# A routed mixture of experts whose block loop is reordered in three places: the planner's frames, the code's arms, and two small blocks' transposes

## The chip, the cores and the metric

The kernel runs on one core of a Trainium2 chip. The metric is device time of the whole program in microseconds (us). PE is the matmul engine, PEld its weight loads, DVE the vector engine, ACT the scalar engine, POOL GpSimd, SP the engine that issues most DMAs.

## What is computed

```python
# attention: b=8 batches, 12 heads, 448 rows, 64 columns
scores = scale * np.matmul(q, k.transpose(0, 1, 3, 2)) - np.log(S)
attn = 1.0 / (1.0 + np.exp(-scores))
x = rows_of(np.matmul(attn, v))          # 3584 x 768
# experts: 8 of them, 768 -> 1024 -> 768
do_compute = x @ w_skip > 0
xc = x[do_compute]
e_idx = np.argmax(xc @ w_gate, axis=1)   # one expert for each row
gate_w = softmax(xc @ w_gate)[e_idx]
for e in range(E):
    h = np.maximum(xc[e_idx == e] @ w1[e], 0.0)
    y[e_idx == e] = gate_w * (h @ w2[e])
out = x.copy(); out[do_compute] = xc + y
```

With these inputs 1333 rows go to experts, by the reference's own arithmetic 36, 12, 0, 158, 17, 675, 19 and 416 to experts 0 to 7.

## The kernel before

**Stages.** The first 300 us are the attention and the routing, batch by batch; while the last batches run, the weights of the fullest expert (expert 7) are loaded and split. Two blocks of expert 7 run outside a loop, a planner on DVE (L857 to L1031) works out a table of the other blocks meanwhile, and a loop over that table (L1443) runs them one after the other.

**Blocks.** A full block is 128 rows of one expert. Its matmuls take each weight as the sum of two parts: `wh`, a rounded copy that ACT makes (`hi1`, `hi2`), and `wl`, the remainder that DVE and POOL make (`lo1`, `lo2`). Activations are split in the same way (`hh` on ACT L523, `hl` on DVE L524). So a full block has 98 matmuls of one pass. A small block has at most 64 rows and multiplies with the unsplit weights `raw`: `half` (33 to 64 rows) and `few` (up to 32). An expert whose rows fill no full block is called pure, and has one small block and no other. An expert with full blocks is called mixed, and its remainder, if it has one, is a small block as well, ahead of its first full block.

**Two sets of weights.** `raw` holds the next expert, `wh` and `wl` the one whose full blocks run. The last full block of a mixed expert is a splitting block: it multiplies with the old `wh` and `wl`, and as each is read for the last time, it overwrites it with the parts of `raw`. It is of type SPLIT where the next mixed expert has a remainder, which still needs `raw`, and of type LAST where it has none, and then issues the loads of the next `raw` itself. A small block issues the loads of the next `raw` behind its own matmuls (`load_w1` behind the first product, `load_w2` behind the second), from SP. Pure experts are put one to a frame behind the full blocks, so that each finds its `raw` loaded.

**Frames.** The planner gives every full block a number, `slot`. A frame is a slot's remainder block, full block and pure block in this order. `gs` is the slot of a mixed expert's first full block, `prk` a pure expert's place among the pure ones, and `pf` the frame that a pure expert gets.

**Rows ahead.** While a block runs, its rows are in `xc`, those of the next in `xn`, and those of the one behind that are gathered from the output in DRAM to `xg` by POOL (`fetch`). A block ends in `finish` (DVE writes `ys`), `put` (POOL: a tiny `jk` that reads `xg`, and then the scatter of `ys` to the output) and `advance` (DVE copies `xn` to `xc`, `xg` to `xn`, and the records). A gather waits until the scatter ahead of it has landed, `jk` and `advance` wait until the gather has landed. `turn_x` transposes `xn` on PE in two halves of three matmuls, into `pxt[0]` and `pxt[1]`; `ready_x` splits them.

**Arms.** The loop's body reads the block's type on every engine and branches to one of five arms, each with its own code on each engine. With all the steps in the arms written out in order by hand (`manual_schedule`), the order on each engine is that of the code.

**Blocks of this run.** In the trace of before the loop runs: full, SPLIT (both expert 7), half (remainder of 5), full, half (expert 0), full, few (1), full, few (4), full, few (6), SPLIT (all full ones of expert 5), few (remainder of 3), full (3). That is the order that the planner's lines give for the counts above.

Of the kernel before, what the change touches and what calls it, by code (L numbers as in the profile page):

```python
# [15 lines left out]
ALU = mybir.AluOpType  # L16
AX = mybir.AxisListType
# [7 lines left out]
def kernel(  # L25
# [451 lines left out]
    def turn_x(x, h, px):  # L477
        for j in range(3):
            i = 3 * h + j
            nc.tensor.transpose(  # L480
                px[:, j * P : (j + 1) * P], x[:, i * P : (i + 1) * P], ident
            )
# [326 lines left out]
    xn = rows_pool.tile([P, DM], F32, name="xn")  # L809
# [25 lines left out]
    FULL, SPLIT, LAST, FEW, HALF = range(5)  # L835
# [8 lines left out]
    def small(name, w=NE, dt=F32):  # L844
        return area(w, dt)

    def dep(t, e):
        return t.unsqueeze(2).to_broadcast([P, NE, NE]) if e else t.unsqueeze(1).to_broadcast([P, NE, NE])
# [6 lines left out]
    V = nc.vector  # L855
# [28 lines left out]
    mixed = small("mixed")  # L884
# [13 lines left out]
    bef = area(NE * NE).rearrange("p (e f) -> p e f", e=NE)  # L898
# [8 lines left out]
        gemm2(j, hh0, hl0, py)  # L907


    tmp = small("tmp")  # L910
    V.scalar_tensor_tensor(tmp, gs, 3.0, mixed, op0=ALU.is_le, op1=ALU.mult)
    soon = small("soon", 1)
    V.tensor_reduce(soon, tmp, axis=AX.X, op=ALU.add)
    late = small("late")
    V.scalar_tensor_tensor(late, gs, 3.0, mixed, op0=ALU.is_gt, op1=ALU.mult)
    push = small("push")
    V.tensor_tensor(push, gs, mrk, op=ALU.subtract)
    V.tensor_scalar(push, push, soon, -4.0, op0=ALU.add, op1=ALU.add)
    V.tensor_tensor(bef, dep(push, 0), dep(prk, 1), op=ALU.is_le)
    V.tensor_tensor(bef, bef, dep(late, 0), op=ALU.mult)  # L920
    pf = small("pf")
    V.tensor_reduce(pf, bef, axis=AX.X, op=ALU.add)
    V.scalar_tensor_tensor(pf, pf, 3.0, prk, op0=ALU.add, op1=ALU.add)


# [337 lines left out]
    def few(i):  # L1263

        nx = next_expert(ds(i + 2, 1))

        def quarter(dst, g, n, a, w, j, most):
            nc.tensor.matmul(  # L1268
                dst[g * SM : (g + 1) * SM, :n],
                a,  # L1270
                w,
                start=(j == 0),
                stop=(j == most - 1),
                tile_position=(0, g * SM),
            )

        Q1 = FF // 4
        for j in range(NK1):
            for g in range(4):
                s = slice((g % 2) * Q1, (g % 2 + 1) * Q1)  # L1280
                quarter(ph[0], g, Q1, xf[:, j, :SM], raw1[j][g // 2][:, s], j, NK1)
        turned = (pht[0], ph[1])
        parts = [slice(c * P, (c + 1) * P) for c in range(2)]
        for s in parts:
            nc.scalar.activation(hs[:, s], ph[0][:, s], AF.Relu)
        for j in range(NK1):
            for h in range(2):
                load_w1(j, h, nx)
        fetch()
        turn_x(xn, 0, pxt[0])  # L1290
        ht4 = ht[:, : 8 * SM].rearrange("p (c g t) -> p c g t", c=2, g=4)
        for s, p in zip(parts, turned):
            nc.tensor.transpose(p[:, :P], hs[:, s], ident)
        for s, p in zip(parts, turned):
            nc.scalar.activation(ht[:, s], p[:, :P], AF.Copy)
        turn_x(xn, 1, pxt[1])
        shift(pool)
        ready_x()

        for n, j in enumerate((0, 2, 1, 3)):  # L1300
            for g in range(4):
                o, h = g // 2, g % 2
                m = j + h * (NK2 // 2)
                quarter(
                    py[:, 0, :],
                    g,
                    H2,
                    ht4[:, j % 2, 2 * h + j // 2, :],
                    raw2[m][:, o * H2 : (o + 1) * H2],
                    n,  # L1310
                    NK2 // 2,
                )
        for j in range(NK2 // 2):
            for g in range(2):
                load_w2(j + g * (NK2 // 2), nx)
        for g in range(4):
            o, m = divmod(g, 2)
            s = slice(o * H2, (o + 1) * H2)
            nc.vector.scalar_tensor_tensor(
                ys[:SM, s],  # L1320
                py[g * SM : (g + 1) * SM, 0, :H2],
                recs[:SM, 0, 0:1],
                (ys if m else xc)[:SM, s],
                op0=ALU.mult,
                op1=ALU.add,
            )
        put(SM)
        advance()

    def half(i):  # L1330
# [21 lines left out]
            for h in range(2):  # L1352
                load_w1(j, h, nx)
        fetch()
        turn_x(xn, 0, pxt[0])
        for c in range(4):
            nc.tensor.transpose(
                turned[c // 2][:, (c % 2) * P : (c % 2 + 1) * P],
# [2 lines left out]
            )  # L1361
        for s, p in zip(parts, turned):
            nc.scalar.activation(ht[:, s], p[:, : 2 * P], AF.Copy)
        turn_x(xn, 1, pxt[1])
        ready_x()
        shift(dve)

# [38 lines left out]
    def choose(kind, i, todo):  # L1406

        if len(todo) == 1:
            with tc.manual_schedule():
                arms[todo[0]](i)  # L1410
            return
        n = 1 if FULL in todo else (len(todo) + 1) // 2
        with tc.If(kind < todo[n]) as c:
            choose(kind, i, todo[:n])
        with c.Else():
            choose(kind, i, todo[n:])
# [31 lines left out]
```

## Time and profile before

| | |
|---|---|
| median of 3 runs | 582.51 us (580.81 to 585.02) |
| profiled execution | 585.59 us, its span 583.9 us |
| granted clock, mean | 0.979 |
| PE busy | 530.6 us, 91% of the span |
| DMA, mean over the span | 174 GB/s |

The profiled execution is 3.1 us above the median; its span leaves 1.7 us of it out. The loop's first block starts at 346.24 us of the span, its last matmul ends at 569.35 us. Times below are of this one execution.

### The profile page before, as it was taken

The page shows a single profiled execution, that of the slowest core. Times are in us where ns is not written, and L with a number is a line of the kernel's source. Part 1 is how long each engine was busy: PE and PEld are TensorE (multiplying, and loading weights), DVE is VectorE, ACT ScalarE, POOL GpSimd, SP SyncE. Part 2 cuts the span into 40 slices and gives each one's busy share as a digit, 9 for nine tenths or more (in the row PEclk, how much of TensorE's full clock was granted, in tenths as well). Part 3 has the DMA queues.
Part 4 walks back from the last instruction along what each step waited for, and adds up shares of the span by engine and source line. Part 5 has one row for each costly group of instructions (what it writes and reads, how often), then busy time and mean ns, then how long its engine had stood idle before and what let it go on. Part 6 is the DMA issues. An engine that isn't in the chain of part 4 may idle for free.

```text
span 583.9 us, 15458 instructions
## 1 busy us (share of the span) xinstructions
PE 530.6 (91%) x4803; PEld 347.7 (60%) x4804; DVE 322.7 (55%) x716; ACT 273.0 (47%) x473; POOL 263.0 (45%) x377
## 2 busy tenths in 40 slices
PE   7989999999999999888889999799999999997790
PEld 6654544544445454443448898575859686776490
DVE  3555748466485666857948621386341435439732
ACT  4766666766667576664551122182222222257120
POOL 2524543353433536669774222086332334347630
PEclk9999999999999999999999999799999999998896
DMA  8899797687966869999951229119385869593100
GB/s 213 173 250 200 153 191 163 136 159 152 203 147 138 176 139 213 218 216 218 234 113 18 98 63 363 38 59 317 135 294 203 275 217 314 213 331 132 35 14 28
DMA packets 138361, 101.46 MB, mean 174 GB/s; under 512 B 98132, under 2 KB 113764, under 8 KB 138304
## 3 DMA queue, kind: packets, MB, share of 16 engines
q1 hardware_dynamic: 132240, 91.58, 61.4%
q0 software_dynamic: 4032, 8.65, 4.8%
q10 hardware_dynamic: 2032, 0.50, 0.4%
q8 instruction: 32, 0.52, 0.4%
q14 instruction: 25, 0.20, 0.1%
HBM read 92.64 MB, written 17.86 MB: 189 GB/s over the span
## 4 chain that ended last, share of the span: by engine, by line
PE 54%; DMA 15%; issue 10%; DVE 7%; ACT 6%; POOL 3%; SPq 2%; ACTq 0%; DVEq 0%; POOLq 0%
PE s L209 15%; PE pa L237 13%; PE py L531 7%; PE ph L504 6%; DMA out_dram<-ys,rp 5%; ACT at L229 5%; DMA xg<-out_dram,rp 5%; PE b_ph L504 3%; PE b_py L531 3%; DMA out_dram<-y 2%; PE pl L277 1%; SPq L260 1%; PE ph L1268 1%; DMA wr<-in_moe_w_dram 1%; SPq L169 1%
## 5 line engine op out<-in xcount | busy, mean ns | idle before, releaser
L229 ACT ACTIVATE at<-s,bias 128x896 f32<-128x896 f32 x192 | 172.3, 913 | 97.3 <-PE s L209 96.7
L209 PE MATMUL s<-x 64*64 64x448 f32 (+1 forms) x1536 | 166.1, 498 | 14.4 <-ACT at L229 4.7
L237 PE MATMUL pa<-at,v 64*64 64x448 f32 (+1 forms) x1536 | 163.6, 491 | 0.0
L176 POOL COPY kq<-kq 32x896 f32<-32x896 f32 (+1 forms) x96 | 87.8, 914 | 120.3 <-DMA kq<-in_q_dram 80.8
L209 PEld LDWEIGHTS s<-x 64*64 64x64 f32 x1536 | 79.1, 191 | 75.3 <-issue 30.4
L237 PEld LDWEIGHTS pa<-at,v 64*64 64x64 f32 x1536 | 60.7, 133 | 56.0 <-issue 49.8
L194 DVE STREAM_TRANSPOSE x<-kq 128x448 f32<-128x448 f32 x94 | 81.5, 941 | 8.0 <-POOL kq L176 7.2
L247 DVE TENSOR_TENSOR xt<-xt,pa 128x448 f32<-128x448 f32 x48 | 29.7, 618 | 67.6 <-ACT xt L642 62.5
L407 POOL DMA_INDIRECT lst<-rec,idx x32 | 31.4, 982 | 28.0 <-DVE idx L402 14.9
L513 ACT ACTIVATE hs<-ph 128x512 f32<-128x512 f32 x16 | 9.5, 596 | 62.6 <-PE ph L504 61.2
L531 PE MATMUL py<-wh,hl 128*128 128x384 f32 x128 | 33.3, 341 | 4.4 <-DVE hl L524 4.4
L252 DVE STREAM_TRANSPOSE y<-xt 128x448 f32<-128x448 f32 x48 | 31.0, 645 | 10.8 <-DMA out_dram<-y 9.4
L504 PE MATMUL ph<-wh,xh 128*128 128x512 f32 x96 | 29.7, 411 | 6.2 <-issue 5.7
L531 PE MATMUL py<-wh,hh 128*128 128x384 f32 x128 | 34.2, 348 | 0.0
L531 PE MATMUL py<-wl,hh 128*128 128x384 f32 x128 | 32.8, 337 | 0.0
L474 POOL TENSOR_TENSOR wl<-wr,wh 128x384 fp32r<-128x384 f32 (+1 forms) x28 | 31.0, 1133 | 3.0 <-DVE wh L473 1.6
L547 POOL DMA_INDIRECT xg<-out_dram,rp x14 | 14.8, 1056 | 38.8 <-DMA out_dram<-ys,rp 36.8
L504 PE MATMUL ph<-wl,xh 128*128 128x512 f32 x96 | 30.7, 411 | 0.0
L524 DVE TENSOR_TENSOR hl<-pht,hh 128x512 fp32r<-128x512 f32 x16 | 11.1, 691 | 33.1 <-ACT hh L523 28.1
L504 PE MATMUL ph<-wh,xl 128*128 128x512 f32 x96 | 27.9, 399 | 0.0
L1185 POOL TENSOR_TENSOR jk<-ys,xg 128x2 f32<-128x2 f32 (+2 forms) x14 | 4.6, 328 | 51.5 <-DVE ys L542 38.0
L504 PEld LDWEIGHTS ph<-wh,xh 128*128 128x128 f32 x96 | 18.3, 195 | 14.1 <-issue 10.4
(263 smaller groups left out, 734.2 us busy)
## 6 DMA issues: line engine op xcount, KB each, us to landing
raw<-in_moe_w_dram SPq DMA_DIRECT2D x84, 256.0 KB
raw<-in_moe_w_dram SPq DMA_DIRECT2D x56, 384.0 KB
v<-in_v_dram SPq DMA_DIRECT2D x48, 256.0 KB
out_dram<-y SPq DMA_DIRECT2D x192, 56.0 KB
kq<-in_k_dram SPq DMA_DIRECT2D x46, 224.0 KB
kq<-in_q_dram SPq DMA_DIRECT2D x46, 224.0 KB
wr<-in_moe_w_dram SPq DMA_DIRECT2D x12, 256.0 KB
wr<-in_moe_w_dram SPq DMA_DIRECT2D x16, 192.0 KB
```

Of the source, the lines that this page charges most:

```text
L176: nc.gpsimd.tensor_copy(a[BT:, :, :, :BT], a[:BT, :, :, BT:])
L194: nc.vector.transpose(xs[:, n].rearrange("p (r j) -> p j r", j=NJ), t.rearrange("p (j d) -> p j d", d=D)[:, :, :BT],)
L209: nc.tensor.matmul(sc[m * D : (m + 1) * D, j, : qs.stop - qs.start], xs[r, 0, first::NR7], xs[r, 1, qs], start=True, stop=True,)
L229: nc.scalar.activation(at[:, :, :n], sc[:, :, :n], AF.Sigmoid, bias=bias, scale=SCALE)
L237: nc.tensor.matmul(pa[j * D : (j + 1) * D, r, qs], vt[rs, j, r + c if c < 3 else 3 * (1 - r), :], at[rs, j, : qs.stop - qs.start], start=( ...
L247: nc.vector.tensor_tensor(x, x, pa[:, 1, :S], op=ALU.add)
L252: nc.vector.transpose(y, xts[b][:, hp, :])
L407: put = nc.gpsimd.indirect_dma_start(out=lst[:, :], out_offset=bass.IndirectOffsetOnAxis(ap=idx[:, c : c + 1], axis=0), in_=rec[:, c, :], ...
L474: nc.gpsimd.tensor_tensor(lo, r, hi, op=ALU.subtract)
L504: nc.tensor.matmul(ph[h], a[:, j * P : (j + 1) * P], w[j][h], start=(n == 0), stop=(n == len(t) - 1),)
L531: nc.tensor.matmul(py[:, o, :H2], a[h][:, js], w[j][:, o * H2 : (o + 1) * H2], start=(j == 0 and n == 0), stop=(j == NK2 - 1 and n == 2),)
L547: nc.gpsimd.indirect_dma_start(out=dst, out_offset=None, in_=out[0:rows, :], in_offset=bass.IndirectOffsetOnAxis(ap=idx, axis=0), bounds_c ...
```

## The change

**Planner.** Before, a pure expert goes into the frame `3 + prk` plus one for every mixed expert (that starts behind slot 3) whose first slot has been reached by then, so that frames are skipped one at a time: the count `pf` is a sum. After, each such mixed expert pushes pure experts by an amount `away` of its own, which is worked out so that none stands in the frame ahead of a splitting block, and the largest push counts: `pf` is a maximum. With the counts above, experts 0, 1, 4 and 6 stand in frames 4, 5, 6 and 7 before, and in 4, 5, 6 and 9 after. The loop's blocks are then: full, SPLIT, half (5), full, half (0), full, few (1), full, few (4), full, SPLIT, few (3), full (3), few (6). The small block of expert 6 leaves the place ahead of the second splitting block and becomes the last block. The planner has five DVE instructions more.

**Arms.** The type is compared in another order, and the true side is always placed next. The arms stand in each engine's code as FULL, SPLIT, few, half, LAST before, and as SPLIT, FULL, LAST, few, half after; the loop's end stands behind them all.

**Transposes.** In `few` and `half` both halves of `turn_x` stand ahead of the transposes of `hs`, instead of one ahead and one behind.

```diff
+    at4 = small("at4")
+    V.scalar_tensor_tensor(at4, gs, 4.0, mixed, op0=ALU.is_equal, op1=ALU.mult)
+    held = small("held", 1)
+    V.tensor_reduce(held, at4, axis=AX.X, op=ALU.add)
+    V.scalar_tensor_tensor(held, soon, 2.0, held, op0=ALU.mult, op1=ALU.add)
     push = small("push")
-    V.tensor_tensor(push, gs, mrk, op=ALU.subtract)
-    V.tensor_scalar(push, push, soon, -4.0, op0=ALU.add, op1=ALU.add)
+    V.scalar_tensor_tensor(push, mrk, -2.0, gs, op0=ALU.mult, op1=ALU.add)
+    V.tensor_scalar(push, push, held, -5.0, op0=ALU.add, op1=ALU.add)
+    away = small("away")
+    V.scalar_tensor_tensor(away, push, -1.0, gs, op0=ALU.mult, op1=ALU.add)
+    V.scalar_tensor_tensor(away, away, -3.0, late, op0=ALU.add, op1=ALU.mult)
     V.tensor_tensor(bef, dep(push, 0), dep(prk, 1), op=ALU.is_le)
-    V.tensor_tensor(bef, bef, dep(late, 0), op=ALU.mult)
+    V.tensor_tensor(bef, bef, dep(away, 0), op=ALU.mult)
     pf = small("pf")
-    V.tensor_reduce(pf, bef, axis=AX.X, op=ALU.add)
+    V.tensor_reduce(pf, bef, axis=AX.X, op=ALU.max)
     V.scalar_tensor_tensor(pf, pf, 3.0, prk, op0=ALU.add, op1=ALU.add)
...
         fetch()
-        turn_x(xn, 0, pxt[0])
+        for h in range(2):
+            turn_x(xn, h, pxt[h])
...
             nc.scalar.activation(ht[:, s], p[:, :P], AF.Copy)
-        turn_x(xn, 1, pxt[1])
...
-        n = 1 if FULL in todo else (len(todo) + 1) // 2
-        with tc.If(kind < todo[n]) as c:
+        if todo[0] == FULL:
+
+            with tc.If(kind > FULL, preferred_fallthrough_block=True) as c:
+                choose(kind, i, todo[1:])
+            with c.Else():
+                choose(kind, i, todo[:1])
+            return
+        n = (len(todo) + 1) // 2
+        with tc.If(kind < todo[n], preferred_fallthrough_block=True) as c:
             choose(kind, i, todo[:n])
```

On PE, at the end of the first arm in the code and the start of the next (`py` is the second product, `ph` the first; L1413 is the branch). Before, this is FULL and then SPLIT:

```order
L531 MATMUL py<-wh_7_123,hh_4361 128x384 x2
L531 MATMUL py<-wl_7_131,hh_4361 128x384 x2
L531 MATMUL py<-wh_7_123,hl_4363 128x384 x2
L1413 UNCONDITIONAL_BRANCH
L1413 COMPARE_AND_BRANCH x2
L504 MATMUL ph_4372<-wh_0_0_92,xh 128x512
L504 MATMUL ph_4372<-wl_0_0_104,xh 128x512
L504 MATMUL ph_4372<-wh_1_0_94,xh 128x512
```

After, the same place holds SPLIT's end and FULL's start, and SPLIT is what the loop's head runs into without a taken branch:

```order
L531 MATMUL py<-wh_7_123,hh_4366 128x384 x2
L531 MATMUL py<-wl_7_131,hh_4366 128x384 x2
L531 MATMUL py<-wh_7_123,hl_4368 128x384 x2
L1429 UNCONDITIONAL_BRANCH
L504 MATMUL ph_4377<-wh_0_0_92,xh 128x512
L504 MATMUL ph_4377<-wh_1_0_94,xh 128x512
L504 MATMUL ph_4377<-wh_2_0_96,xh 128x512
```

Two arms changed places; a SPLIT multiplies by `wh` and `wl` in turn, a FULL by all `wh` first. The whole code of LAST now stands between FULL and `few`, where SPLIT stood.

On PE in `few`, between its two products (`pxt` are the halves of the next rows, `pht` and `ph_4373` the transposes of `hs`, L1268 the products). Before:

```order
L480 MATMUL pxt_4294<-ident,xn 128x128 x3
L1293 REGISTER_ALU
L1293 MATMUL pht<-ident,hs 128x128
L1293 REGISTER_ALU
L1293 MATMUL ph_4373<-ident,hs 128x128
L480 MATMUL pxt_4295<-ident,xn 128x128 x3
L1268 ISA
L1268 MATMUL py<-raw_0_4352,ht 32x384
```

After:

```order
L480 MATMUL pxt_4299<-ident,xn 128x128 x3
L480 MATMUL pxt_4300<-ident,xn 128x128 x3
L1303 REGISTER_ALU
L1303 MATMUL pht<-ident,hs 128x128
L1303 REGISTER_ALU
L1303 MATMUL ph_4378<-ident,hs 128x128
L1277 ISA
L1277 MATMUL py<-raw_0_4357,ht 32x384
```

The second half's three transposes moved from behind the two of `hs` to ahead of them, in `half` likewise.

## Rows read from the trace of the kernel before

**Rows 1.** The page: busy us, share of the span, instructions.

```profile
PE 530.6 (91%) x4803; PEld 347.7 (60%) x4804; DVE 322.7 (55%) x716; ACT 273.0 (47%) x473; POOL 263.0 (45%) x377
```

**Rows 2.** Windows: stretch, length, busy us (instructions) by engine, PEclk, DMA share, GB/s.

```profile
369.29:390.19 20.90, 20.90 (x99) 18.36 (x99) 11.14 (x16) 13.42 (x26) 8.86 (x11) 0.87 0.09 25
369.29:375.17 5.88, 5.88 (x14) 4.63 (x15) 0.00 (x0) 0.00 (x0) 0.00 (x0) 0.52 0.05 16
480.46:488.44 7.98, 7.00 (x90) 4.15 (x89) 4.01 (x11) 2.69 (x12) 2.20 (x7) 1.00 0.73 225
507.02:515.40 8.38, 7.00 (x89) 4.15 (x89) 4.08 (x12) 2.69 (x12) 2.21 (x7) 1.00 0.64 208
515.40:538.65 23.25, 19.91 (x98) 17.63 (x98) 16.66 (x25) 14.05 (x27) 15.69 (x21) 0.93 0.67 237
538.65:550.93 12.28, 8.07 (x89) 4.10 (x89) 10.58 (x16) 4.31 (x15) 8.63 (x12) 0.86 0.08 32
550.93:569.35 18.42, 18.42 (x102) 16.45 (x98) 6.77 (x17) 4.14 (x12) 6.46 (x16) 1.00 0.08 18
569.35:583.90 14.55, 0.00 (x0) 0.00 (x0) 2.98 (x9) 0.00 (x0) 1.40 (x2) 0.62 0.07 28
```

**Rows 3.** Timeline of PE: start, us, what, in brackets idle ahead and releaser.

```profile
369.29 0.77 PE L504 MATMUL ph<-wh,xh 128*128 128x512 f32 x1 [4.74 <-issue]
...
403.78 0.47 PE L504 MATMUL ph<-wh,xh 128*128 128x512 f32 x1 [0.92 <-issue]
...
484.66 0.30 PE L1293 MATMUL pht<-ident,hs 128*128 128x128 f32 x1 [0.92 <-ACT hs L1285]
...
529.05 1.01 PE L531 MATMUL py<-wh,hl 128*128 128x384 f32 x2 [3.34 <-DVE hl L524]
...
545.66 0.87 PE L480 MATMUL pxt<-ident,xn 128*128 128x128 f32 x3 [4.21 <-DVE recs L1197]
```

**Rows 4.** Timeline of POOL, block ahead of the second splitting block, and end.

```profile
515.49 1.02 POOL L547 DMA_INDIRECT xg<-out_dram,rp  x1 [3.27 <-DMA out_dram<-ys,rp]
...
521.46 0.59 POOL L1185 TENSOR_TENSOR jk<-ys,xg 32x2 f32<-32x2 f32 x1 [2.42 <-DMA xg<-out_dram,rp]
...
571.59 1.17 POOL L557 DMA_INDIRECT out_dram<-ys,rp  x1 [0.55 <-issue]
```

**Rows 5.** Timeline of DVE in and behind the two splitting blocks.

```profile
379.62 0.69 DVE L524 TENSOR_TENSOR hl<-pht,hh 128x512 fp32r<-128x512 f32 x1 [0.17 <-ACT hh L523]
...
395.77 0.16 DVE L1197 COPY recs<-rn 128x2 f32<-128x2 f32 x1
...
521.45 0.56 DVE L1194 COPY xn<-xg 128x768 f32<-128x768 f32 x1 [2.96 <-DMA xg<-out_dram,rp]
...
525.24 3.04 DVE L1140 TENSOR_TENSOR wl<-raw,wh 128x512 fp32r<-128x512 f32 x3 [2.49 <-PE py L531]
...
542.93 2.58 DVE L1197 COPY recs<-rn 128x2 f32<-128x2 f32 x1
```

**Rows 6.** Groups by form, 500 to 584: a small block's last step on DVE.

```profile
L1319 DVE SCALAR_TENSOR_TENSOR ys<-py,recs,xc 32x384 f32<-32x384 f32 x4 | 2.4, 608 | 3.6 <-PE ph L504 3.0 <-PE py L1268 0.5
```

**Rows 7.** Chain that ended last: one scatter and the gather behind it, start, us.

```profile
410.28 3.77 DMA out_dram<-ys,rp
...
414.86 3.88 DMA xg<-out_dram,rp
```

**Rows 8.** Timeline of DVE in the planner's code.

```profile
321.77 0.56 DVE L490 TENSOR_TENSOR b<-b_px,b 128x384 fp32r<-128x384 f32 x1 [0.39 <-ACT b L486]
323.15 0.56 DVE L490 TENSOR_TENSOR b<-b_px,b 128x384 fp32r<-128x384 f32 x1 [0.83 <-ACT b L486]
```

**Rows 9.** DMA queues, 361 to 373, then all queues of 403.5 to 581: packets, MB.

```profile
q8 instruction: 2, 0.03, 1.1%
...
q1 hardware_dynamic: 12701, 28.34, 45.6%
q0 software_dynamic: 2048, 5.46, 9.8%
```

More of the change, by code (lines that the diff above doesn't have):

```diff
@@ L1354, in half @@
         fetch()
-        turn_x(xn, 0, pxt[0])
+        for h in range(2):
+            turn_x(xn, h, pxt[h])
         for c in range(4):
@@ L1363, in half @@
             nc.scalar.activation(ht[:, s], p[:, : 2 * P], AF.Copy)
-        turn_x(xn, 1, pxt[1])
         ready_x()
```

## The prediction

> **What bounds the kernel now.** I read the page first: PE is busy for 91% of the span [rows 1], so time can come only from the stretches in which PE waits or runs at the lower clock. The windows by block show where these are [rows 2]. The reader is to compare like with like. A full block takes 18.42 us with PE busy throughout. A splitting block has the same 98 matmuls and takes 20.90 the first time and 23.25 the second. A small block takes 7.98 in the middle of the run, 8.38 ahead of the second splitting block and 12.28 behind it. Behind the last matmul 14.55 us pass. The timeline of PE then names the waits [rows 3]: 4.74 us for nothing that the profile shows at the first switch from FULL to SPLIT, 3.34 for `hl` in the second SPLIT, 4.21 for DVE in the small block behind it. [...]
>
> The wait for `hl` has its cause in the block ahead. That block is `few` for expert 6. Its gather waits for the full block's scatter (POOL idle 3.27 us) and is issued at 515.49, after PE has already begun SPLIT; it lands ahead of `jk` at 521.46 [rows 4]. DVE can copy `xn` only then, at 521.45, and reaches SPLIT's first remainder at 525.24, which takes 3.04 us for three; `hl` stands behind them [rows 5]. PE comes to need `hl` 10.3 us into SPLIT (529.05 less 3.34). In the first SPLIT, with a full block ahead, DVE made `hl` at 379.62 and was idle ahead of it [rows 5], and PE had no wait between 369.29 and 390.19 [rows 2].
>
> **The planner's part.** It takes `few` (6) from ahead of the second SPLIT and puts it last.
>
> Out of its old place go 8.38 us, and into the last place come 7.98, the price of a `few` between full blocks [rows 2]: -0.4. Its weights are loaded from the `few` ahead of it (expert 3) and over the full block; that is 7.98 + 18.42 = 26.4 us from start to start, as between the small blocks of before, which did not wait for `raw` (the `few` at 507.02 has PE busy for 7.00 us, as the one at 480.46 [rows 2]), so I cost the load at nothing. If that cover were gone, PE would wait for the load's remainder.
>
> SPLIT then follows a full block. Its floor is the full block's 18.42; the first SPLIT's 20.90 is that and 2.5 us of half clock, which its first 14 matmuls bear out: 5.88 us at a mean clock of 0.52 are 3.1 at full clock [rows 2]. I take 18.4 instead of 23.25: -4.85. The weights that it splits are those that the `few` two blocks ahead has loaded, over a whole full block.
>
> The small block behind it still waits for DVE's `advance`. In the first case DVE reached the last of the copies that PE waits for at 395.77, 5.6 us after SPLIT's end; in the second that copy itself took 2.58 us at 542.93 [rows 5] and PE went on at 545.66 [rows 3], 7.0 us after SPLIT's end at 538.65. With the first case's delay the wait falls from 4.2 to about 3.1: -1.1. The reordered transposes give some back here: three more matmuls (as long as the first three, 0.87 us at half clock [rows 3]) stand between the end of the wait and `hs`, and the copies of `ht` no longer have them as cover. I take +0.4. Together -0.7, with bounds of -4.2 (no wait) and +0.4.
>
> At the end, `few` finishes in four DVE steps of 608 ns [rows 6] where the full block has two: +1.2. The scatter that closes the kernel is started 2.24 us behind the last matmul at 571.59 [rows 4], and 12.3 us follow it in either case. One chain could be later: the full block's scatter (2.24 us behind its last matmul), its landing 3.77, 0.8 to the next issue, the gather 3.88 [rows 7], `jk`: 10.7 us, against 7.98 + 2.5 = 10.5 for the `few` itself. It is level, so I add nothing and keep +2 as its bound.
>
> Sum of the planner's part: -0.4 - 4.85 - 0.7 + 1.2 = -4.75 us. The five added DVE instructions, each about 0.2 us, stand ahead of two DVE waits for ACT of 0.39 and 0.83 us [rows 8], which hide them; without that cover they would be 1 us.
>
> **The arms' part.** At the end of the first full block each engine jumps from FULL over all the other arms to the loop's end, back to the head, and into SPLIT. PE stood still for 4.74 us, and then lost 2.5 to the clock. In the window around it the instruction queue q8 carried two packets; from 403.5 to 581, over eleven blocks, there is no packet on any instruction queue [rows 9]. So code is fetched on first use, and later switches cost nothing. [...]
>
> After the change the jump to the loop's end is as far as before. What changes is that FULL no longer starts the loop's code: the code that is read ahead while FULL runs differs, and one of the two fetches in a row may be done by then. The two prices that the trace has for a switch with a fetch are 4.74 with two and 0.92 at 403.78 with PE's queue as cover [rows 3]. I take the middle, 2.4 us instead of 4.74, and no half clock, since the waits that led to it were 3.34 and longer: -2.3 - 2.5 = -4.8. Against it stand new first jumps: over SPLIT at the loop's entry, and into `half`, which now stands behind three arms; the second takes the place of the 0.92 at `half`'s end. I price the entry at 0.9. Sum -3.9, with bounds of -7.2 (the stall gone) and +4.7 (kept, and another like it at the entry).
>
> **The transposes' part.** In a `few` between full blocks PE waits 0.92 us for `hs` [rows 3], and the moved matmuls fill that; but they covered the copies of `ht` behind it. A tenth each way, three times; in the two `half` blocks PE doesn't wait there, and it may lose 0.2 each. Sum +0.1.
>
> **Total.** -4.75 - 3.9 + 0.1 = -8.55 us on the profiled execution, 585.6 to 577.0. That execution lies 3.1 us above the median of 582.5; the difference carries over, so the forecast is 582.5 - 8.55, or **574.0 us**.
>
> **Rivals.**
> First, the fetch stall stays whole or moves to another switch. The jump's distance speaks for it, the changed order of the arms against. Then only the planner's part is left, and an entry stall of up to 2 us eats of it: 577 to 580, which I put at 578.
>
> Second, the gain is passed on: SPLIT ends 4.85 us earlier, but DVE and POOL still have their remainders to make, so that the small block behind waits 5 us or more, and the end chain adds its 2. That gives the planner's part about -2; with the other parts as forecast, 576.7. For it speaks that DVE is busy 16.66 us of SPLIT's 23.25 and 10.58 of the next 12.28 [rows 2]; against it, that the first SPLIT did the same work in 20.90 and its next block waited less.
>
> Third, slower: LAST's code, which never runs here, now lies between FULL and the small arms, and the pages that the loop touches no longer stay. Then each of the ten switches between FULL or SPLIT and a small arm from the first `half` on pays 0.92 to 4.74 us [rows 3]: +9.2 to +47, and with the planner's gain 587 to 625. It decides from 0.5 us a switch. [...] Against it: FULL and the loop's end were further apart than that before, and no packet was fetched [rows 9].
>
> Fourth, the change doesn't do what it says: if expert 6 kept its frame, the arms' and transposes' parts alone would give 578.7. By the planner's lines it moves, so I give it little.
>
> **How the numbers follow.** Forecast (570.5 to 576.5) 0.55; first rival 0.22; second 0.13; third 0.05; fourth 0.02; the stall gone and more than that, below 570.5, 0.03. About 1% (5.8 us) is what a measurement of this kernel can tell from no change, so faster means under 576.7. The forecast, the deep case and half of the second rival lie there, and a tenth of the first: 0.66. Slower is the third rival: 0.05. The rest, 0.29, is the same. The range runs from 569.5 to 580.5: below by a stall that is gone, above by the first rival with its entry stall.
>
> **What the changed profile would show.** The planner's part is right if the second SPLIT follows a full block and takes 18 to 19 us without a wait for `hl`, the `few` behind it waits 2.5 to 3.5 us, and a `few` stands last, with some 16 us from its last matmul to the end. The arms' part is right if PE's wait ahead of the first SPLIT is 1 to 3 us at clock 1.00 and the loop's first block starts within 1 us of the last matmul ahead of it. It is wrong if 4 us or more and a half clock still stand there, or if a new wait on nothing shown stands ahead of the first `half`. Instruction packets behind the first small block would show the third rival.

## The result, and the profile after

The changed kernel takes 584.75 us (median of 20 runs, 581.21 to 586.67), the kernel before 581.55 (20 runs): a ratio of 1.0043, 95% interval 1.0023 to 1.0064. By the ratio it is 2.5 us slower, where 8.55 us of gain were forecast. Ratios, here and below, compare the fast executions of both kernels and are not quotients of the medians. The profiled execution took 585.88 us (span 584.0), as long as the profiled one of before (585.59), which lies above all 20 runs of that kernel. So the two traces have to be compared block by block, not by their spans.

The page, busy time by engine [rows 1]:

```profile
PE 533.3 (91%) x4803; PEld 350.7 (60%) x4804; DVE 324.4 (56%) x721; ACT 272.9 (47%) x473; POOL 264.2 (45%) x377
```

The windows of the blocks that the sum speaks of: first SPLIT with the wait behind it, first half, then from the full block ahead of the second SPLIT to the end [rows 2]. Columns: stretch, length, busy us (instructions) by engine, PEclk, DMA share, GB/s.

```profile
368.44:391.08 22.64, 19.96 (x98) 17.59 (x99) 13.48 (x19) 15.46 (x28) 11.60 (x13) 0.92 0.09 28
391.08:403.40 12.32, 12.18 (x67) 6.62 (x67) 8.80 (x13) 3.23 (x13) 9.95 (x15) 1.00 0.76 238
486.83:506.87 20.04, 18.48 (x99) 16.55 (x99) 7.08 (x17) 4.14 (x12) 7.83 (x17) 1.00 0.76 277
506.87:525.11 18.24, 18.24 (x99) 16.35 (x99) 14.12 (x25) 13.43 (x26) 10.30 (x13) 1.00 0.14 44
525.11:536.93 11.82, 8.65 (x90) 5.08 (x89) 10.75 (x13) 4.58 (x15) 10.32 (x13) 0.86 0.77 240
536.93:559.08 22.15, 20.23 (x101) 17.86 (x98) 6.95 (x17) 4.23 (x13) 7.79 (x17) 0.92 0.50 186
559.08:567.00 7.92, 7.13 (x89) 3.92 (x88) 4.01 (x11) 2.69 (x12) 3.51 (x9) 1.00 0.13 50
567.00:584.00 17.00, 0.00 (x0) 0.00 (x0) 4.16 (x11) 0.00 (x0) 2.97 (x7) 0.59 0.04 11
```

The planner did what it should: the second SPLIT takes 18.24 us instead of 23.25. But the full block two blocks on takes 22.15 instead of 18.42, and 17.00 us instead of 14.55 lie behind the last matmul. From the second SPLIT's neighbour to the end nothing is won.

PE's waits [rows 3], from its timeline (idle ahead and releaser in brackets):

```profile
368.44 0.59 PE L504 MATMUL ph<-wh,xh 128*128 128x512 f32 x1 [4.45 <-issue]
...
391.08 1.04 PE L1344 MATMUL ph<-raw,xf 128*64 128x512 f32 x3 [2.68 <-ACT wh L1152]
...
498.66 0.62 PE L531 MATMUL py<-wh,hl 128*128 128x384 f32 x2 [1.55 <-DVE hl L524]
...
531.00 0.85 PE L480 MATMUL pxt<-ident,xn 128*128 128x128 f32 x6 [2.87 <-DVE recs L1206]
...
549.20 0.74 PE L531 MATMUL py<-wh,hl 128*128 128x384 f32 x2 [1.93 <-DVE hl L524]
```

The wait at the first switch from FULL to SPLIT is there as before, 4.45 against 4.74. A new one of 2.68 us stands ahead of the first half. The profile puts it down to ACT, but in the instruction records PE's jump into half's code starts at 387.06 and takes 3.54 us. A releaser is the last semaphore that came, and a jump has none; an instruction packet moves within that jump, and the experiments below bear it out. At the first switch PE's jump starts at 360.73 and takes 5.89 us. The DMA queues (packets, MB, share of 16 engines), in 360.5 to 364.1, in 364.1 to 367, in 386.9 to 390.7 (the jump into half, q8 alone), and in 403.5 to 581 [rows 9]:

```profile
q1 hardware_dynamic: 522, 1.44, 103.1%
...
q1 hardware_dynamic: 63, 0.14, 13.7%
q8 instruction: 1, 0.02, 2.3%
...
q8 instruction: 1, 0.02, 1.5%
...
q1 hardware_dynamic: 12863, 28.66, 46.1%
q0 software_dynamic: 2021, 5.42, 9.3%
```

Before, q8 carried two packets at the first switch; now it carries one, as the changed order of the code was expected to bring. But that one starts 3.5 us behind the jump, at 364.24, when the loads of the next expert's weights (399 GB/s until then) run out. From 403.5 on there is again no instruction packet.

DVE in the small block behind the second SPLIT and in the full block behind that:

```profile
540.12 0.83 DVE L1202 COPY xc<-xn 128x384 f32<-128x384 f32 x2
545.02 0.56 DVE L1203 COPY xn<-xg 128x768 f32<-128x768 f32 x1 [4.06 <-DMA xg<-out_dram,rp]
...
546.13 0.17 DVE L1207 CAST rid<-recs 128x3 int32<-128x3 f32 x1
548.45 0.69 DVE L524 TENSOR_TENSOR hl<-pht,hh 128x512 fp32r<-128x512 f32 x1 [2.15 <-issue]
```

POOL there, first the scatter of SPLIT's rows:

```profile
530.95 1.03 POOL L557 DMA_INDIRECT out_dram<-ys,rp  x1 [0.27 <-issue]
...
538.33 1.03 POOL L547 DMA_INDIRECT xg<-out_dram,rp  x1 [2.21 <-DMA out_dram<-ys,rp]
...
545.03 0.59 POOL L1194 TENSOR_TENSOR jk<-ys,xg 32x2 f32<-32x2 f32 x1 [3.14 <-DMA xg<-out_dram,rp]
```

The chain reads so: the gather is issued 7.4 us behind the scatter, and its data are there 6.7 us later. DVE stands in `advance` for it (4.06), then needs 2.15 us for nothing shown, in which the instruction records have its own jump through the loop's end and head (546.16 to 547.98), and only then makes the `hl` that PE has been waiting for. Behind this wait PE runs at a lower clock (0.50 between 549.54 and 552.96, 0.92 in the mean of the block).

### The profile page after: what moved, and what is told of

Its sections match the earlier page's. It is cut to its first block, busy times and chain, and to the rows that moved or that the text cites. A ratio compares the mean times of both kernels' runs of the same rounds, so it can differ in the third digit from the quotient of the medians.

```text
span 584.0 us, 15455 instructions
## 1 busy us (share of the span) xinstructions
PE 533.3 (91%) x4803; PEld 350.7 (60%) x4804; DVE 324.4 (56%) x721; ACT 272.9 (47%) x473; POOL 264.2 (45%) x377
## 4 chain that ended last, share of the span: by engine, by line
PE 45%; DMA 22%; issue 12%; DVE 7%; ACT 4%; POOL 4%; SPq 3%; POOLq 1%; ACTq 0%; DVEq 0%
PE s L209 13%; PE pa L237 12%; DMA out_dram<-ys,rp 8%; DMA xg<-out_dram,rp 6%; PE py L531 6%; PE ph L504 5%; ACT at L229 4%; PE b_ph L504 3%; PE b_py L531 3%; DMA out_dram<-y 3%; SPq L260 2%; DVE x L194 1%; PE pl L277 1%; POOL kq L176 1%; DVE xc L1202 1%
## 5 line engine op out<-in xcount | busy, mean ns | idle before, releaser
L209 PE MATMUL s<-x 64*64 64x448 f32 (+1 forms) x1536 | 169.2, 502 | 11.4 <-ACT at L229 3.7
L237 PE MATMUL pa<-at,v 64*64 64x448 f32 (+1 forms) x1536 | 166.4, 494 | 0.0
L237 PEld LDWEIGHTS pa<-at,v 64*64 64x64 f32 x1536 | 62.3, 134 | 56.7 <-issue 49.3
L542 DVE SCALAR_TENSOR_TENSOR ys<-py,recs,xc 128x384 f32<-128x384 f32 x16 | 9.1, 613 | 32.1 <-PE py L531 27.3
```

The lines of the kernel that those rows point to most:

```text
L209: nc.tensor.matmul(sc[m * D : (m + 1) * D, j, : qs.stop - qs.start], xs[r, 0, first::NR7], xs[r, 1, qs], start=True, stop=True,)
L237: nc.tensor.matmul(pa[j * D : (j + 1) * D, r, qs], vt[rs, j, r + c if c < 3 else 3 * (1 - r), :], at[rs, j, : qs.stop - qs.start], start=( ...
```

## The experiments

Ratios are to the kernel before on the same chip, with 95% intervals. Block lengths run from a block's first matmul to that of the next.

**The parts one by one.** Each kernel is the kernel before with the named hunks of the diff and no others.

> The kernel before with the planner's part alone, the arms and transposes as they were. Theory: the 4.9 us that the second SPLIT gains are given back by the full block and the small block behind it and by the longer end, so this is within 1 us of the kernel before (581 to 583). Rival A (the arms cost what the changed kernel lost): the planner's part has its forecast gain, 576 to 578. Rival B (the planner's part is itself the loss): 584 to 586.

> The kernel before with the arms' part alone. Theory: the wait at the first switch from FULL to SPLIT stays between 4 and 5 us and a new one of 2 to 3 us stands ahead of the first half, so 582 to 585. Rival A (the arms are the whole loss and hide the planner's gain): 586 to 588. Rival B: no difference, 581 to 582.

> The kernel before with the transposes' part alone. Theory and rivals A and B: within 0.5 us of the kernel before (581 to 582). Rival C (the transposes are at fault): 583 or more, with PE waiting for the copies of ht in the small blocks.

> The changed kernel with the arms put back as they were before. Theory: the planner's part gives about nothing, so 581 to 583, and the changed kernel lies 2 to 3 us above it. Rival A: 576 to 578. Rival B: as the changed kernel, 584 to 586.

| kernel | median us | ratio |
|---|---|---|
| planner_alone | 579.13 | 0.9948 (0.9919 to 0.9976) |
| arms_alone | 584.91 | 1.0049 (1.0018 to 1.0081) |
| turns_alone | 582.12 | 1.0006 (0.9974 to 1.0037) |
| planner_and_turns | 579.18 | 0.9961 (0.9929 to 0.9992) |

Neither theory nor rival A is right alone. The planner's part gives 0.52%, 3.0 us, not nothing; the arms' part costs 0.49%, 2.9 us, as its theory had it, with waits of 4.39 us ahead of SPLIT and 2.42 ahead of half. The transposes do nothing that can be measured. (A later measurement of planner_and_turns, below, finds less gain.) The windows of planner_alone, second SPLIT and the two blocks behind it:

```profile
502.61:520.85 18.24, 18.24 (x99) 16.35 (x98) 14.02 (x25) 13.43 (x26) 10.28 (x13) 1.00 0.14 44
520.85:531.93 11.08, 8.22 (x90) 4.21 (x89) 10.38 (x11) 3.85 (x9) 9.57 (x10) 0.85 0.71 222
531.93:552.23 20.30, 18.64 (x103) 16.34 (x99) 8.35 (x20) 5.12 (x18) 8.52 (x21) 1.00 0.59 222
```

The same give-back, but smaller: the full block takes 20.30, not 22.15.

The arms' loss is found between the start of the loop's first block and that of its fourth, the full block behind the first half. With the arms of before this takes 57.5 (before), 56.7 (turns_alone), 56.0 (planner_alone) and 55.2 us (planner_and_turns), with the new ones 57.7 (changed kernel), 58.2 (arms_alone) and 59.2 (planner_and_arms, below): means of 56.4 and 58.4.

**Do the parts add?**

> The planner's and the arms' part without the transposes'. Theory (the parts add): the planner gives 3 us, the arms cost 3, so 581 to 583. Rival (the arms cost more when the planner's part is there, as the changed kernel's 584.75 against 579.2 without the arms suggests): 584 to 586.

581.38 us against 580.60: 1.0029 (0.9991 to 1.0066). The interval holds both answers. Open at this point.

**Where the code stands.** The arms' order is set by the nesting of the comparisons alone. full_last:

```diff
-            choose(kind, i, todo[:n])
+            choose(kind, i, yes)
...
-        choose(entry(TYP, ds(i + 2, 1), mybir.ALL_ENGINES, HALF), i, range(len(arms)))
+        tree = (HALF, (FULL, (FEW, (LAST, SPLIT, LAST), FEW), FULL), HALF)
+        choose(entry(TYP, ds(i + 2, 1), mybir.ALL_ENGINES, HALF), i, tree)
```

A triple is a bound, the arms for `kind < bound` and the others (with FULL, which is 0, or in the next two kernels a negative bound, the test is `kind > -bound`).

> The planner's and the transposes' part with the arms in the order SPLIT, half, LAST, few, FULL, so that FULL's end runs into the loop's end, and the jump out of it goes only back to the head, with SPLIT behind it. Theory (the wait ahead of the first SPLIT is for code that a far jump has to fetch): that wait falls from 4.2 to 4.7 us to under 1.5, SPLIT runs without a half clock (18.4 us), the first half waits under 1 us; the entry jump into FULL may now cost up to 3.5 us. In sum 574 to 578. Rival A (the wait only moves to the loop's entry): 578 to 580. Rival B (the wait doesn't hang on the distance): 4 us or more still ahead of SPLIT, 579 or more.

587.40 us, 1.0146 (1.0092 to 1.0199). PE's waits for nothing shown, from its timeline:

```profile
343.40 0.47 PE L504 MATMUL ph<-wh,xh 128*128 128x512 f32 x1 [2.39 <-issue]
...
396.58 0.70 PE L504 MATMUL ph<-wh,xh 128*128 128x512 f32 x2 [2.27 <-issue]
...
415.77 0.74 PE L1344 MATMUL ph<-raw,xf 128*64 128x512 f32 x2 [0.79 <-issue]
...
430.91 0.47 PE L504 MATMUL ph<-wh,xh 128*128 128x512 f32 x1 [2.75 <-issue]
...
461.40 0.77 PE L504 MATMUL ph<-wh,xh 128*128 128x512 f32 x1 [4.42 <-issue]
```

Ahead of the first SPLIT there is no wait, and SPLIT takes 18.24 us: the theory of the jump's target holds there. But the entry pays 2.39 and three of the next four switches into FULL pay 2.3 to 4.4, with six packets on q8 between 390 and 460. The theory and rival A priced this too low. It is what the prediction's third rival supposed, code that doesn't stay: absent in the changed kernel, where eleven blocks from 403.5 on fetch no packet, and present with another order of the same arms, in these six packets (0.10 MB, so 16 KB each).

half_third moves LAST, which never runs here, behind the small arms; half_third_full_first has FULL, SPLIT, half, few, LAST.

```diff
+        tree = (FULL, (LAST, SPLIT, (-FEW, HALF, (-LAST, FEW, LAST))), FULL)
```

```diff
+        tree = (LAST, (SPLIT, FULL, SPLIT), (-FEW, HALF, (-LAST, FEW, LAST)))
```

> The changed kernel with its five arms in the order SPLIT, FULL, half, few, LAST: the arm that never runs here is moved from between FULL and the small arms to behind them. Theory (what the changed arms lose is the code fetch ahead of the first half): the wait of 2.4 to 2.7 us ahead of the first half goes or falls under 1 us, the one ahead of the first SPLIT stays at 4.3 to 4.5, so 1.5 to 2.5 us under the changed kernel, a ratio to the kernel before of 0.998 to 1.002. Rival (that fetch is no more than a symptom, the loss lies in the later blocks): 1.004 as the changed kernel. Rival of the other sign (moving code costs fetches elsewhere, as with FULL last): above 1.006, with waits for nothing shown at other switches.

> The planner's and the transposes' part with the arms in the order FULL, SPLIT, half, few, LAST. Theory: as with the arms of before (0.996 of the kernel before), the wait ahead of SPLIT 4.2 to 4.7 us and none ahead of half; at half's end the wait of up to 0.9 us may go or grow, as the loop's end lies one small arm further away. Rival: a new fetch of 2 us or more at half's end, 0.999.

583.94 us, 1.0017 (0.9986 to 1.0048), and 583.65, 1.0036 (1.0011 to 1.0061). The first lies in its range; the second is a miss, above its theory and above its rival, whose new fetch at half's end came. In both the wait ahead of half is gone, and one at half's end takes its place. PE in half_third_full_first:

```profile
400.30 0.47 PE L504 MATMUL ph<-wh,xh 128*128 128x512 f32 x1 [2.90 <-issue]
```

So half's 2.68 us are a code fetch (in the changed kernel the packet of q8 starts at 388.27, inside the jump of 387.06 to 390.61), whatever releaser the profile names, and an order can move it but has not removed it. With the arms of before a fetch lies at half's end (its packet starts at 399.97 in the kernel before), behind half's last matmuls, and 0 to 0.92 us of it show.

**Is the fetch slow, or does it queue?** The second product's weights of the first load are left out, and zeros written in their place.

```diff
         for j in range(NK2):
-            load_w2(j, nx)
+            dve.memset(raw2[j], 0.0)
```

> The changed kernel with the second product's weights of the first load left out (zeros are written in their place, so expert 5 is computed with zeros), so that the DMA queues are empty when PE jumps out of the first full block. Theory (the one code fetch that is left stands behind the weights in the DMA queues): its packet starts 1 to 1.5 us after the jump instead of 3.5, and the wait ahead of SPLIT falls from 4.4 to 2 to 3 us. Rival (the fetch is slow by itself): 4 us or more. The wait of 2.7 us ahead of the first half stays by both.

> The planner's and the transposes' part with the arms of before, and with the second product's weights of the first load left out and zeros in their place (expert 5 is computed with zeros). Theory (two fetches in a row, each about 2.3 us when the DMA queues are empty, against one in the changed arms): the wait ahead of the first SPLIT is 3.3 to 4 us, that is 1.5 to 2 us longer than the 1.82 of the changed arms without that load. Rival (the old arms too wait for the queues alone): 1.8 us as in the changed arms.

One execution each, 577.45 and 573.48 us. PE in half_load, first SPLIT and first half:

```profile
360.09 0.47 PE L504 MATMUL ph<-wh,xh 128*128 128x512 f32 x1 [1.82 <-issue]
...
382.48 1.04 PE L1344 MATMUL ph<-raw,xf 128*64 128x512 f32 x3 [2.39 <-ACT wh L1152]
```

PE in half_load_old_arms, first SPLIT:

```profile
363.92 0.47 PE L504 MATMUL ph<-wh,xh 128*128 128x512 f32 x1 [2.24 <-issue]
```

With empty queues the packet starts 1.1 us behind the jump (jump at 355.0, packet at 356.1) and the wait falls from 4.45 to 1.82, less than the 2 to 3 expected: beside the weights this packet starts only as they run out, 3.5 us behind the jump. Not every packet does. In the kernel before, the first of the two starts 1.4 us behind the jump (361.29, 362.73), beside 399 GB/s, and only the second (364.95) as the weights run out; why one gets through and the other doesn't, no run shows. My figure for the old arms, 3.3 to 4, was wrong: 2.24, nearer the rival. There one of the two packets starts at 357.3, ahead of the jump at 358.42. So the old arms lose little by their second fetch, 0.4 us between these two executions; with the queues full both orders wait alike, 4.2 to 4.7 us in the kernels with the parts of the old order and 4.3 to 4.5 in those of the new. The change had almost nothing to win at this place.

**Why does the full block give time back?** few3_no_load takes expert 6's loads out of the small block behind the second SPLIT, so that expert 6 is computed with expert 3's weights.

```diff
+    V.memset(slots[0:1, 13:14], 0)
```

> The planner's and the transposes' part, with the loads that the small block of expert 3 issues left out (the expert behind it then multiplies with expert 3's weights). Theory (the loads of expert 6 slow the scatter and the gather of that block, and so the full block behind it): that full block takes 18.4 to 19.5 us instead of 20.3 to 22.2 and doesn't wait for hl; the time is 576 to 578 against 579.2. Rival (the second SPLIT's remainders on DVE and POOL delay it): the block stays over 20 us, no change of time.

575.70 us against 580.60: 0.9925 (0.9888 to 0.9962), where planner_and_turns, on another chip, had 0.9961; these two intervals overlap, so the block's length has to decide. The window of the full block, then POOL's gather ahead of it and the `jk` behind it:

```profile
531.36:549.69 18.33, 18.33 (x101) 16.45 (x98) 7.57 (x19) 5.12 (x18) 7.89 (x20) 1.00 0.06 15
```

```profile
532.42 1.03 POOL L547 DMA_INDIRECT xg<-out_dram,rp  x1 [0.64 <-issue]
...
536.14 0.18 POOL L1195 TENSOR_TENSOR jk<-ys,xg 32x2 f32<-32x2 f32 x1
```

The gather's data are used 3.7 us behind its issue instead of 6.7, and the block is back at 18.33. The loads slow the gather; SPLIT's remainders, which this kernel has as well, do not delay the block. With the loads in place the block took 20.05 to 22.15 us in the profiles of planner_alone, the two measurements of planner_and_turns and the changed kernel. One profile is an exception: in half_load_old_arms it took 18.42 with the loads, and the small block ahead of it 12.85 instead of 10.3 to 11.9, so the wait can also fall there.

late_advance takes the copies that wait for the gather out of the small block's end, and puts them into the next block behind its first `hl`.

```diff
+    def arrive():
+        nc.vector.tensor_copy(xn, xg)
+        nc.vector.tensor_copy(recs[:, 2, 0:2], rn[:, 0:2])
+        nc.vector.tensor_copy(rid, recs[:, :, 1])
...
         split_h(0, pht[0], hh, hl)
+        arrive()
```

> The planner's and the transposes' part, and the copies that wait for the gather (xn from xg, the last record, the row numbers) are taken out of the small block's end on DVE and stand in the next block behind the first hl; every block makes them there, which repeats them where they were made already, and two copies ahead of the loop fill xg and rn. Theory (the full block behind a small one waits for hl because DVE stands in order behind the gather, and behind its own loop overhead): the full blocks behind the small ones take 18.3 to 18.9 us instead of up to 22, none waits for hl; 0.988 to 0.992 of the kernel before. Rival (the chain of scatter and gather itself is the bound, and the wait only moves from hl to xn): as without this edit, 0.996, with waits at L480 of the same size.

617.28 us, 1.0620 (1.0584 to 1.0655): a failure as a kernel. All full blocks behind small ones take 18.6 to 18.7 us without a wait for `hl`, as the theory has it. But in half and few the repeated copies make PE wait for `xn`, 2 to 11 us each time.

> As late_advance, but the three copies stand in the full and splitting blocks alone, and no longer in half and few (in this run a full block follows every few, so nothing is lost by it; a small block behind a few would lack its rows). Theory (the full block behind a small one waits for hl only because DVE stands in order behind the gather): the small blocks take 8.0 and 10 to 11 us as with the planner's and the transposes' part, the full blocks behind them 18.3 to 18.8 without a wait for hl; 0.988 to 0.993 of the kernel before, against 0.996 without this edit. Rival (the wait moves to xn, at L480, or to the next small block): 0.995 to 0.998.

> The same edit on the kernel before with the transposes' part alone, so with expert 6 still ahead of the second SPLIT. Theory (SPLIT waited for hl for the same reason, DVE in order behind the gather): SPLIT takes 19 to 20.5 us instead of 23, without a wait of 3 us for hl, so this is 0.992 to 0.996 of the kernel before, and the planner's part is worth only 1 to 2 us on top. Rival (SPLIT's remainders are late by themselves): SPLIT stays over 22 us, 0.998 to 1.001, and the planner's part is worth 4 to 5 us on top.

> The same edit on the whole changed kernel. Theory (the changed arms cost their code fetch ahead of half and nothing in the later blocks): 1.5 to 3 us above late_full, with the later blocks as long as there. Rival (the arms also cost time in the later blocks, as the changed kernel's distance of 5 us to the kernel without them could say): 4 us or more above late_full, with longer blocks behind the first half.

591.44, 590.43 and 590.47 us; 1.0176 (1.0145 to 1.0207), 1.0167 (1.0137 to 1.0197), 1.0155 (1.0121 to 1.0188). Slower again, now mainly in the small blocks behind a SPLIT. The three copies take DVE 2.9 us in the middle of SPLIT. The gather is issued 16.6 us into the block instead of 15.4, and DVE's remainders are late as well: two of them take 7.93 us beside POOL's, 1.83 in planner_and_turns. PE in late_full, ahead of the transposes in the first half:

```profile
399.40 1.51 PE L480 MATMUL pxt<-ident,xn 128*128 128x128 f32 x6 [5.61 <-DVE recs L1208]
```

But the window of the second SPLIT in late_full_old_plan, where expert 6 still stands ahead of it, says what the edit was made for:

```profile
517.87:536.50 18.63, 18.53 (x98) 16.37 (x98) 15.84 (x25) 13.56 (x26) 13.61 (x19) 1.00 0.86 304
```

18.63 us, where turns_alone, the same kernel without the edit, has 23.0. The wait for `hl` in SPLIT and the later one in the full block are one and the same: DVE in order behind the gather. The planner's part moves it from one block to the other. The medians of the three bear out neither theory nor rival: late_full lies 1.0 us above late_full_old_plan, so with this edit the planner's part gains nothing that can be measured, and late_full_new_arms lies 1.0 under late_full, so the arms cost nothing there.

late_plain is late_full without the copies in SPLIT (`if not last: arrive()`).

> As late_full, with the three copies in the full blocks alone and no longer in SPLIT (in this run a full block follows every few). Theory (DVE's order behind the gather is what the blocks behind small ones wait for, and late_full lost its time to the copies in SPLIT, where they hold up the fetch): the first half and the small block behind the second SPLIT are back at 12.8 and 10 to 11 us, all full blocks take 18.7, so 1 to 3 us under the kernel without the edit: 0.988 to 0.994 of the kernel before. Rival (the copies cost the full blocks as much as they save): 0.995 to 0.998.

> The same edit on the whole changed kernel. Theory (the arms cost the code fetch ahead of half and nothing in the later blocks): 1.5 to 3 us above late_plain. Rival: 4 us or more above it.

> The same kernel as planner_and_turns, beside the two others on one chip: 0.993 to 0.999 of the kernel before by both, and late_plain 1 to 3 us under it by the theory, level with it by the rival.

| kernel, one chip | median us | ratio |
|---|---|---|
| late_plain | 574.06 | 0.9925 (0.9895 to 0.9955) |
| late_plain_new_arms | 574.93 | 0.9939 (0.9909 to 0.9968) |
| planner_and_turns_again | 577.85 | 0.9998 (0.9969 to 1.0026) |

late_plain is the best version: 3.8 us under planner_and_turns by the medians, more than the theory's 1 to 3. It holds for orders of blocks in which a full block follows every `few`. DVE in it, around the same place as above:

```profile
536.65 0.17 DVE L1350 COPY recs<-sv 128x4 f32<-128x4 f32 x1
539.32 0.69 DVE L524 TENSOR_TENSOR hl<-pht,hh 128x512 fp32r<-128x512 f32 x1 [2.50 <-ACT hh L523]
540.08 0.56 DVE L1212 COPY xn<-xg 128x768 f32<-128x768 f32 x1
```

`hl` now waits for nothing but ACT, and the full block takes 18.83. The new arms cost 0.9 us on top here, under the theory's 1.5 to 3, and the intervals overlap, so this pair doesn't show that they cost anything; the rival's 4 us or more is excluded. The stretch to the loop's fourth block takes 57.4 us in both.

planner_and_turns_again is a miss: 0.9998, where both sides expected 0.993 to 0.999. The same kernel had 0.9961 on the other chip, and the intervals overlap. So the size of the planner's gain is not settled; the three ratios that have it without the new arms give 3.0, 2.3 and 0.1 us.

## Why the prediction was wrong

**Planner's part, step by step.** Forecast, then planner_alone's profile (and the changed kernel's).

| term | forecast | planner_alone | changed kernel |
|---|---|---|---|
| expert 6's block to the end | -0.4 | -0.4 | -0.5 |
| second SPLIT | -4.85 | -5.0 | -5.0 |
| small block behind it | -0.7 | -1.2 | -0.5 |
| full block behind that | not in the sum | +1.9 | +3.7 |
| behind the last matmul | +1.2 | +2.7 | +2.5 |
| sum | -4.75 | -2.0 | +0.2 |

The measured lengths are the windows above, less those of before [rows 2]; in planner_alone expert 6's block ends at 560.19, 7.96 us after its start, and the span at 577.4. SPLIT, the small block and the moved block came as worked out. The step that failed is "Its weights are loaded from the `few` ahead of it (expert 3) and over the full block; [...] so I cost the load at nothing". PE does not wait for `raw` (busy for 7.13 of the 7.92 us of expert 6's block, 7.00 of 7.98 before), so as a wait for weights that was right. But the loads run beside the gather (99.1% of the 16 engines' time for q1 between 538.2 and 545 in the changed kernel), whose data are used 6.7 us behind its issue with them and 3.7 without (few3_no_load); DVE stands in order behind the gather, and that had a price. The second rival spoke of a gain that is passed on, to the small block; it was passed on one block further. The signs that the prediction named for this part came (SPLIT 18.24, the `few` behind it waiting 2.87, a `few` last, though with 17.0 us behind it instead of some 16), but none of them looked at the full block behind.

The end was forecast at +1.2, with up to 2 us more if a chain of scatter and gather came later; 1.3 to 1.5 more came, but not from that chain: POOL's wait for the gather ends at 568.86 in the changed kernel's instruction records, ahead of DVE's last finishing step. DVE's first finishing step and the last scatter's issue in the changed kernel, from the two timelines:

```profile
568.68 0.60 DVE L1328 SCALAR_TENSOR_TENSOR ys<-py,recs,xc 32x384 f32<-32x384 f32 x1 [2.77 <-POOL rp L1192]
```

```profile
572.09 1.10 POOL L557 DMA_INDIRECT out_dram<-ys,rp  x1 [0.55 <-issue]
```

DVE starts 1.68 us behind the last matmul's recorded end (567.00), in the kernel before 0.23. The profile names POOL's `rp`. In three kernels DVE's wait ends within 0.02 us of the end of PE's drain instruction instead (568.40, 561.65 and 559.34 in the changed kernel, planner_alone and planner_and_turns), so I take it that the small block's products come later than the record says. That is argued, not tested.

**Arms' part.** "One of the two fetches in a row may be done by then": one packet fewer, as thought. The traces show code that is read ahead: in the kernel before a packet of q8 starts at 342.80, with PE busy for all of the 3.00 us behind it, and in half_load_old_arms one starts at 357.3, ahead of the jump at 358.42. The step that failed is the price put on that, "I take the middle, 2.4 us instead of 4.74, and no half clock". The wait stayed at 4.45, since the one fetch that is left starts only as the weights run out (3.5 us behind the jump, 1.1 in half_load), and the clock fell again (0.92 in this SPLIT with 19.96 us of PE time, 1.00 with 18.24 in the second). That every wait under 3.34 us leaves the clock alone, on which "no half clock" rests, no run shows: behind 1.82 us in half_load the clock was 0.72, behind 2.24 us in half_load_old_arms 1.00. The other failed price is "the second takes the place of the 0.92 at `half`'s end": 2.68 instead of 0.92. The loop's entry, priced at 0.9, had no wait. Both signs of being wrong came, the 4 us with a lower clock and the new wait ahead of the first half. The forecast of -3.9 is +2.9 alone (0.18% to 0.81%), and the traces place 2.0 of it, by the two means, in the loop's first three blocks; in the later pair, late_plain and late_plain_new_arms, the whole loss was 0.9, which can't be told from nothing. The bounds of that term, -7.2 to +4.7, held it; the chance given to its bad side, 0.27 with the first and the third rival, did not do it justice.

**Transposes.** +0.1 forecast, 1.0006 measured: right within what can be told.

**First, third and fourth rival.** The first rival had the arms' mechanism right, a stall that stays and another that appears at another switch, but let the planner keep its whole gain (578). The third's repeated fetches did not come in the changed kernel, and the planner's move, which the fourth doubted, did happen.

**What stays open.** The parts alone give -3.0 + 2.9, about nothing, and the changed kernel is at +2.5. So of the 11 us between forecast and result some 8.5 are placed in these two parts by the runs of each alone, and 2.5 are not; the later runs give less to both, 0.1 us of gain and 0.9 of loss. The difference lies inside the intervals together; that the blocks behind the small ones differ from execution to execution (below) may be part of it, which is not shown.

## What to carry to other kernels

Before costing a transfer at nothing, ask not only whether its data come in time, but what small transfers run beside it and which engine stands in order behind one of those: a copy that waits for a gather belongs behind the work that the next block needs first. A releaser that the profile names is the last semaphore, so a wait just behind a jump is checked against the instruction queue's packets before it is believed. Code that is fetched on first use cost PE 2.3 to 4.7 us here beside busy data queues (2.27 in full_last, 4.74 in the kernel before), 1.8 to 2.7 beside empty or nearly empty ones (1.82 in half_load, 2.68 in the changed kernel), and under 1 where other work was queued ahead of the jump (0.92 at half's end in the kernel before); the order of arms moved such a fetch more easily than it removed it (2.68 ahead of half became 3.44 at its end in half_third and 2.90 in half_third_full_first).

## What the runs showed of the hardware that was not expected

One code fetch of PE cost a wait of 4.45 us with the data queues full (changed kernel) and 1.82 with them empty (half_load). The same full block of the same kernel, the one ahead of the second SPLIT, took 18.20 us in one execution and 22.90 in another. The windows of that block in planner_and_turns, and in planner_and_turns_again:

```profile
481.66:499.86 18.20, 18.20 (x99) 16.58 (x100) 6.74 (x17) 4.50 (x15) 7.74 (x17) 1.00 0.88 314
```

```profile
479.27:502.17 22.90, 20.24 (x98) 18.00 (x99) 7.67 (x19) 5.13 (x18) 7.78 (x17) 0.93 0.69 251
```

The second has a wait of 2.27 us for `hl` and the lower clock behind it. The gather takes as long in both (its data are used 6.4 and 6.5 us behind its issue), but it is issued 5.4 us behind the scatter in the first and 7.1 in the second, so a chain that ends just as it is needed decides the block's length. Why the scatter took longer, no run shows. A wait's length alone did not decide the clock: after 1.82 us in half_load the clock was 0.72 and 0.70 in the two stretches that followed (360.09 to 366), after 2.24 us in half_load_old_arms it stayed at 1.00 (363.92 to 374).
